# Retention, softplus MoE and routed MoE on one core: a third raw buffer inside the ring for the second matrix, all softplus of the second batch in pairs, halves of q in one operation

## The chip, the cores and the metric

The kernel runs on one core of a Trainium2 chip. The metric is device time in microseconds (us), the median of three runs. All times below come from the runs and the profiled execution of the kernel before, unless said otherwise.

## What is computed

Three layers in a row, all float32 at the borders. A retention attention (4 batches, 8 heads, 768 tokens, 64 per head) feeds a dense MoE layer with a softplus (3072 tokens, 512 to 2048 to 512), and this feeds a routed layer with 8 experts, one for each token.

```python
for t in range(S):
    state = gamma * state + einsum('bhd,bhe->bhde', k[:, :, t], v[:, :, t])
    y[:, :, t] = scale * einsum('bhd,bhde->bhe', q[:, :, t], state)
h = x @ w_in
g = maximum(h, 0) + log1p(exp(-abs(h)))
x2 = g @ w_out                                    # w_out is 2048 x 512
expert = argmax(x2 @ w_gate, axis=1)              # then one of 8 experts:
out[mask] = gate[mask] * (maximum(x2[mask] @ w1[e], 0) @ w2[e])
```

## The kernel before

Float32 factors are split into two float16 parts, hi and lo, and a product is three float16 matmuls (hi with hi, hi with lo, lo with hi). The attention goes by 24 chunks of 128 tokens, the dense layer by 8 batches of 384 tokens (three chunks each), the routed layer follows.

**Units.** The dense layer and the attention are written as one sequence of units. A batch has 16 units, one for each 128 columns of `w_in`; unit 16·ph + f is called by that number here. In each unit TensorE (PE) gets, in the order written: 12 matmuls 128x384 of the first matrix for batch ph (`l1_mm`, L890), the attention steps that are due (`at_step`), and 9 matmuls 128x512 of the second matrix (`l2_mm`, L938) for the batch before, four units late (`BACK`). So the second matmuls of batch 0 run in units 20 to 35; unit 20 + kk uses row block kk of `w_out`, and the nine are three token groups times (hi, hi), (hi, lo of `w_out`), (lo, hi). PE's order is the written one. The order on VectorE (DVE), ScalarE (ACT) and SyncE's DMA queue (SP) is set by a scheduler from the program and its priorities; SP is one in-order list (`in_line`).

**The second matrix.** `w_out` comes in eight blocks i = 0 to 7 of 1 MB, each for row blocks 2i and 2i+1. `load_out` (L667) loads a block, in a form that has to be put together from integers, into one of two raw tiles. `decode_out(i)`, written in unit 17 + 2i, first issues the loads up to block i+1, then runs `decode`: DVE L615, L617 and L619 in place on the raw tile, ACT L622 for the hi part, DVE L623 for the lo part. The results lie in `w1t`, which is part 1 of a large buffer (`ring`): per partition 8192 float16 elements of hi (u = 0) and then 8192 of lo (u = 1), a row block taking 512 of each.

**The softplus.** `softplus` (L893 to L920) takes a 128x384 block of PE's result through ACT (abs, relu, exp, ln), DVE L917, ACT L919 and DVE L920. For the units in the table `pairs` two blocks are held together and the later steps run once on 768 columns (DVE L903, L906). Batch 0 is all in pairs, of batch 1 the first four pairs; the other eight units of batch 1 run one by one.

**Attention steps.** For a chunk n: S(n), scores, then on DVE the masks L762 and the rests L764; Y(n), the products with them (L793), then Z, the state (L821 to L824), and on DVE L828, L829, L848 (the state) and L865 (the output's rest), after which SP transposes the output (L866) into `xt`, the input of a later batch. `at_prep` splits a loaded chunk (L713 to L720), and SP transposes it (L722). H is the step L840, once. `STEPS` says in which units of the first two batches the steps are written; in the second batch they are T6, S6, Y6, H6, S7, Y7, S8, Y8, in that order. The first six chunks use an older form (S L746, Y L800, Z L813, then L826 and L860 on DVE).

Of the kernel before, what the change touches and what calls it, by code (L numbers as in the profile page):

```python
# [8 lines left out]
F32 = mybir.dt.float32  # L9
F16 = mybir.dt.float16  # L10
U32 = mybir.dt.uint32
AF = mybir.ActivationFunctionType
ALU = mybir.AluOpType
# [7 lines left out]
P = 128  # L21
H = 8
D = 64
DM = 512
# [6 lines left out]
BT = 384  # L31
NB = NT // BT
CPB = BT // P
NF = FF // P
# [37 lines left out]
def moe_chain(ctx, tc, q, k, v, moe_w_in, moe_w_out, moe2_w_gate, moe2_w1, moe2_w2, cst, cst16, out, dbg=None):  # L72
    nc = tc.nc
# [41 lines left out]
    ring = wpool.tile([P, 4, 32, 512], F16, name="ring")  # L115
# [24 lines left out]
    def in_line(x):  # L140

        if queued[0] is not None:
            tc.add_manual_dep(x, queued[0].name, NOSYNC, reason="order")
        queued[0] = x
# [436 lines left out]
    with ExitStack() as pb, ExitStack() as pa:  # L581
# [5 lines left out]
        dd_stack = at_stack.enter_context(ExitStack())  # L587
        dd_p = dd_stack.enter_context(tc.tile_pool(name="dd", bufs=2, reuse_waits="tile"))
# [3 lines left out]
        def anchor(x):  # L592
            if now[0] is not None:
                tc.add_manual_dep(x.ins, now[0].name, NOSYNC, reason="order")
            return x
# [7 lines left out]
        def tick():  # L603
            for fn, args in events.pop(unit[0], []):
                fn(*args)
            unit[0] += 1
# [20 lines left out]
        BEHIND = {2: 3, 3: 4, 5: 5}  # L627
        LIN, LOUT = 4, 4
        BACK = 4
        STEPS = {0: (1, 2, 4, 5, 7, 9, 9, 11, 13), 1: (1, 3, 5, 6, 7, 9, 10, 13)}  # L630
        FILL = dict(T0=3,S0=2,z0=3,T1=2,S1=4,z1=5,y1=4,S2=6,z2=2)
        flat = ring[:, 2].rearrange("p a b -> p (a b)")
        dbuf = []
# [3 lines left out]
        def ahead(cnt, fn, upto):  # L637
            while cnt[0] < upto:
                fn(cnt[0])
                cnt[0] += 1  # L640

        nload = {"in": [0], "out": [0], "split": [0]}
# [19 lines left out]

        raws = {}

        def load_out(i):
            raws[i] = dd_p.tile([P, 2, DM, 2], U32, tag="raw", name="raw", bufs=2)
            in_line(nc.sync.dma_start(out=raws[i], in_=moe_w_out.rearrange("(k p) (f two) -> p k f two", p=P, two=2)[:, 2 * i:2 * i + 2]).ins)  # L667

        def decode_out(i):
            ahead(nload["out"], load_out, min(NF // 2, i + 2))  # L670
            hl = [w1t[:, u, 2 * i:2 * i + 2, :] for u in range(2)]
            decode(*hl, SWO, raws.pop(i))

# [25 lines left out]
        def at_prep(n):  # L699
            raw = raw_t.pop(n)  # L700
            if n < N32:
                tok_t[n] = raw
                return

            t = tbuf[n % 2]
            vh = at_p.tile([P, H, D], F16, tag="vh", name="vh")
            qv = t[:, 0:1024].rearrange("p (g x) -> p g x", g=4)
            qs = [[qv[:, :, 64 * (3 * half if u == 0 else half + 1):][:, :, 0:64] for half in range(2)] for u in range(2)]
            kv = t[:, 1024:2048].rearrange("p (h u d) -> p h u d", h=H, u=2)
            kl = t[:, 2048:2560].rearrange("p (h d) -> p h d", h=H)  # L710
            vl = t[:, 2560:3072].rearrange("p (h d) -> p h d", h=H)
            q4 = raw[:, 0].rearrange("p (g x) d -> p g x d", g=4)
            for half in range(2):  # L713
                anchor(nc.scalar.activation(out=qs[0][half], in_=q4[:, :, half], func=AF.Copy))
            anchor(nc.scalar.activation(out=kv, in_=raw[:, 2].unsqueeze(2).to_broadcast([P, H, 2, D]), func=AF.Copy))
            anchor(nc.scalar.activation(out=vh, in_=raw[:, 1], func=AF.Copy))
            for half in range(2):
                nc.vector.tensor_tensor(out=qs[1][half], in0=q4[:, :, half], in1=qs[0][half], op=ALU.subtract)
            nc.vector.tensor_tensor(out=kl, in0=raw[:, 2], in1=kv[:, :, 0], op=ALU.subtract)
            nc.vector.tensor_tensor(out=vl, in0=raw[:, 1], in1=vh, op=ALU.subtract)  # L720
            tT = at_p.tile([P, 20, P], F16, tag="tT", name="tT")
            nc.sync.dma_start_transpose(out=tT, in_=t[:, 0:2560])  # L722
            tok_t[n], trn_t[n] = (kv, kl, vh, vl), (tT[:, 0:8], tT[:, 8:16], tT[:, 16:20])
# [148 lines left out]
        spots = [[tbuf[i][:, u * 2 * wide:(u + 1) * 2 * wide] for u in range(2)] for i in range(2)]  # L872
        spots += [[flat[:, NF * BT * (u + 1) - 2 * wide * i:][:, 0:2 * wide] for u in range(2)] for i in (2, 1)]
        spots = [[x.bitcast(F32).rearrange("p (u t) -> p u t", u=2) for x in ar] for ar in spots]
        pairs = {(0, i): spots[3 if i == 7 else (i + 1) % 2] for i in range(8)}
        pairs.update({(1, i): spots[2 + i % 2] for i in range(4)})
        gt = {}
        pend = {}

# [175 lines left out]
        with tc.manual_schedule(engines={nc.tensor.engine}):  # L1055
# [75 lines left out]
            at_scale(CPB + 1)  # L1131
            for ph in range(NB + 1):
                ja, at_ = ph if ph < NB else None, min(ph + 2, NB)
                if ph == 2:
                    dd_stack.close()
                    rw_p = pb.enter_context(tc.tile_pool(name="rw", bufs=3, reuse_waits="tile", side="right"))
                    hl_stack = ExitStack()
                    hl_p = hl_stack.enter_context(tc.tile_pool(name="hl", bufs=2, reuse_waits="tile", side="right"))
                if ph == 7:
                    at_stack.close()  # L1140
                    hl_stack.close()
                    mb = pb.enter_context(tc.tile_pool(name="mb", bufs=2, reuse_waits="tile", side="right"))
                    sl = Slots(mb)
                    rx_p = pb.enter_context(tc.tile_pool(name="rx", bufs=3, reuse_waits="tile", side="right"))
                    late.extend((mb, mb.tile([P, P, 2], F32, tag="tb", name="tb", bufs=1), mb.tile([16, QP, 2], F32, tag="tq", name="tq", bufs=1)))
                if ph == 8:
                    sx_stack.close()
                    sl.pool = pa.enter_context(tc.tile_pool(name="mc", bufs=2, reuse_waits="tile"))
                attn = at_until(at_ * CPB)
                if ph in STEPS:  # L1150
                    attn = [STEPS[ph].count(f) for f in range(NF)]
                for f in range(NF if ph < NB else NF + BACK):
                    tick()
                    now_ = ph * NF + f
                    ph2, f2 = divmod(now_ - BACK, NF)
                    jb = ph2 - 1
                    LGD[0] = 5 if now_ >= NB * NF - 2 else 3
                    if ja is not None:
                        if ja == 0:
                            ahead(din, decode_in, min(NF, f + LIN + 1) // 2)  # L1160
                        l1_mm(ja, f)
                        with tc.high_priority(offset=150):
                            softplus()
                    if ja == 0:
                        if f == 9:
                            others()
                    if ph < 3:
                        ahead(dout, decode_out, min(NF, max(0, now_ - BACK - NF + LOUT + 1)) // 2)
                    for _ in range(attn[f] if ph < NB else 0):
                        at_step()  # L1170
                    if 3 * NF + BACK <= now_ < 7 * NF:
                        ahead(nsp, split, NSP * (now_ + 1 - 3 * NF - BACK) // (4 * NF - BACK))
                    if jb >= 0:
                        l2_mm(jb, f2 * 9, f2 * 9 + 9)
                    if ph2 == 2 and f2 == 10:
                        turns_pick()
                    if ph2 == 2 and f2 == 12:
                        es = experts(range(RING, E))
                        ahead(nload["split"], load_split, 2)
                    if ph2 == 7 and f2 == 7:  # L1180
                        early_pick()
                    if ph2 == 7 and f2 == 11:
                        early_spread()
                        for j in range(-NEARLY, 1 - NEARLY + 2):
                            sl.gather(j)
                    if ph2 == 7 and f2 == 13:
                        for j in range(-NEARLY, 1 - NEARLY + 2):
                            sl.turn(j)
                    if ph2 == 7:
                        if f2 == 5:  # L1190
                            direct = Direct([rw_p, rx_p], experts(range(RING)))
                        if f2 >= 6:
                            direct.at(9 * f2 + 9 - 9 * NF, last[0])
                    if ph2 == 8:
                        if f2 == 3:
                            sl.gather(-1)
                        direct.at(9 * f2 + 9, last[0])
# [158 lines left out]
```

## Time and profile before

| what | us |
|---|---|
| median of 3 runs | 879.53 (879.17 to 880.04) |
| profiled execution, whole time | 878.87 |
| its span, first to last instruction | 877.0 |
| PE busy | 863.2 (98%) |
| VectorE busy | 563.4 (64%) |
| ScalarE busy | 489.0 (56%) |
| PE busy from 100 to 120 / 120 to 140 / 140 to 160 | 18.31 / 18.41 / 20.00 |
| VectorE busy in the same stretches | 20.00 / 18.44 / 19.03 |

The profile is one execution, followed by the hardware profiler. Its whole time is 1.87 us above its span and 0.66 us under the median of the runs. A row of a timeline gives the start, the duration, the engine and the line; a matmul's row ends later than the next begins, since matmuls are pipelined, so times on PE are read here from start to start.

### The profile page before, as it was taken

The numbers are of one execution on the slowest core, as the hardware profiler recorded it, in microseconds if no ns is written. First come the engines' busy times: TensorE is split into PE (matmuls) and PEld (weight loads), VectorE is DVE, ScalarE is ACT, GpSimd is POOL, SyncE is SP. The second block draws the span as 40 slices with busy tenths as digits, with TensorE's granted clock in tenths as the row PEclk, the third lists the DMA queues.
The fourth block names the chain that finished last, engine by engine and source line by source line (L and its number), as shares of the span: only waits on it lengthen the run. The fifth ranks groups of instructions, "written<-read, shape, count | busy, mean of one in ns | idle before, by whom it ended". The sixth has DMA issues, their size and how long they took to land. (4 is left out here: it accounts for less than half of the span.)

```text
span 877.0 us, 17827 instructions
## 1 busy us (share of the span) xinstructions
PE 863.2 (98%) x6541; PEld 469.5 (54%) x6541; DVE 563.4 (64%) x1072; ACT 489.0 (56%) x882; POOL 92.9 (11%) x90
## 2 busy tenths in 40 slices
PE   9999999999999999999999999999999999999996
PEld 6666555555555555556555555544444444444453
DVE  6998998886798798799698645466633332221121
ACT  3688877765776777777676655455333332222220
POOL 0000000001010001001001001201332122212012
PEclk9999999999999999999999999999999999999998
DMA  9991982673779899698886412397699999889992
GB/s 251 252 286 48 222 198 82 148 136 73 181 195 223 209 247 219 192 250 203 229 188 171 124 49 70 107 273 204 153 234 209 208 198 216 225 205 249 300 281 57
DMA packets 281851, 165.87 MB, mean 189 GB/s; under 512 B 246914, under 2 KB 248331, under 8 KB 280738
## 3 DMA queue, kind: packets, MB, share of 16 engines
q1 hardware_dynamic: 276754, 151.49, 71.1%
q0 software_dynamic: 5008, 13.19, 5.3%
q8 instruction: 57, 0.93, 0.5%
q14 instruction: 32, 0.26, 0.1%
HBM read 135.01 MB, written 29.95 MB: 188 GB/s over the span
## 5 line engine op out<-in xcount | busy, mean ns | idle before, releaser
L890 PE MATMUL bank<-xt,ring 128*128 128x384 f16 x1536 | 268.9, 326 | 0.0
L938 PE MATMUL bank<-ring 128*128 128x512 f16 x1104 | 257.2, 379 | 1.6 <-DVE ring L623 1.6
L890 PEld LDWEIGHTS <-ring 128*128 128x128 f16 x1536 | 147.8, 98 | 104.4 <-issue 0.2
L938 PEld LDWEIGHTS <-ring 128*128 128x128 f16 x1152 | 109.4, 98 | 123.2 <-issue 2.3
L452 PE MATMUL h<-ring,xT 128*128 (+4 forms) x840 | 135.4, 361 | 0.0
L452 PE MATMUL bank<-ring,hT 128*128 (+5 forms) x864 | 135.0, 356 | 0.0
L485 ACT ACTIVATE r<-h 128x512 f32<-128x512 f32 (+1 forms) x51 | 30.1, 589 | 128.2 <-PE h L452 122.9
L452 PEld LDWEIGHTS <-hT 128*128 128x128 f16 (+2 forms) x864 | 62.9, 99 | 68.5 <-issue 2.5
L452 PEld LDWEIGHTS <-xT 128*128 128x128 f16 (+2 forms) x840 | 61.6, 98 | 68.7 <-issue 2.3
L910 ACT ACTIVATE a<-bank 128x384 f32<-128x384 f32 x104 | 50.8, 488 | 77.1 <-PE bank L890 77.0
L488 DVE TENSOR_TENSOR hb<-r,hb 128x512 f16<-128x512 f32 (+1 forms) x51 | 35.0, 686 | 83.6 <-ACT hb L487 83.4
L1026 POOL DMA_INDIRECT table<-row,pos x24 | 28.4, 1184 | 554.8 <-DVE pos L1009 512.6
L919 ACT ACTIVATE ring<-r 128x384 f16<-128x384 f32 x104 | 53.7, 519 | 45.7 <-DVE r L917 44.5
L914 DVE TENSOR_SCALAR r<-bank 128x384 f32<-128x384 f32 x96 | 53.1, 553 | 38.9 <-ACT a L910 38.0
L155 DVE SCALAR_TENSOR_TENSOR ring<-raw,ring 128x1024 f16<-128x1024 f32 x32 | 38.6, 1224 | 48.7 <-ACT ring L154 48.7
L920 DVE TENSOR_TENSOR ring<-r,ring 128x384 f16<-128x384 f32 x104 | 57.3, 552 | 18.9 <-ACT ring L919 18.7
L917 DVE SCALAR_TENSOR_TENSOR r<-a,r 128x384 f32<-128x384 f32 x104 | 57.3, 552 | 18.5 <-ACT a L916 18.1
L154 ACT ACTIVATE ring<-raw 128x1024 f16<-128x1024 f32 x32 | 33.0, 1052 | 51.4 <-DMA raw<-in_moe_w_dram 51.3
L916 ACT ACTIVATE a<-a 128x384 f32<-128x384 f32 x104 | 54.1, 520 | 2.2
L915 ACT ACTIVATE a<-a 128x384 f32<-128x384 f32 x104 | 54.0, 519 | 1.9
L522 DVE TENSOR_SCALAR o<-bank,gateT 128x512 f32<-128x512 f32 (+1 forms) x21 | 15.2, 724 | 51.0 <-PE bank L452 51.0
L155 DVE SCALAR_TENSOR_TENSOR hl<-raw,hl 128x1024 f16<-128x1024 f32 x32 | 39.1, 1220 | 4.7 <-ACT hl L154 3.9
(236 smaller groups left out, 936.3 us busy)
## 6 DMA issues: line engine op xcount, KB each, us to landing
ring<-wsp SPq DMA_DIRECT2D x28, 2048.0 KB
raw<-in_moe_w_dram SPq DMA_DIRECT2D x64, 512.0 KB
wsp<-hl SPq DMA_DIRECT2D x32, 512.0 KB
raw<-in_moe_w_out_dram SPq DMA_DIRECT2D x8, 1024.0 KB
ring<-in_moe_w_in_dram SPq DMA_DIRECT2D x7, 1024.0 KB
x2d<-xr SPq DMA_DIRECT2D x24, 256.0 KB
qkv<-in_q_dram SPq DMA_DIRECT2D x18, 256.0 KB
qkv<-in_k_dram SPq DMA_DIRECT2D x18, 256.0 KB
```

The source lines that it names most:

```text
L155: nc.vector.scalar_tensor_tensor(out=lo, in0=raw, scalar=SWE, in1=hi, op0=ALU.mult, op1=ALU.subtract).ins)
L452: ins = nc.tensor.matmul(ps[o, at_:at_ + width], lhsT=lhsT(u), rhs=rhs, start=first and at_ == 0, stop=last and ends).ins
L488: lo = nc.vector.tensor_tensor(out=hb[:, 1, hs], in0=r32, in1=hb[:, 0, hs], op=ALU.subtract)
L890: now[0] = nc.tensor.matmul(ps, lhsT=w0[:, u, kk, fs], rhs=x[:, kk, :], start=(m == 0), stop=(m == 11)).ins
L910: nc.scalar.activation(out=a, in_=ps, func=AF.Abs, scale=C1)
L914: nc.vector.tensor_scalar(out=r, in0=ps, scalar1=C1 * SG, scalar2=0.0, op0=ALU.mult, op1=ALU.max)
L915: nc.scalar.activation(out=a, in_=a, func=AF.Exp, scale=-1.0)
L916: nc.scalar.activation(out=a, in_=a, func=AF.Ln, bias=1.0)
L917: nc.vector.scalar_tensor_tensor(out=r, in0=a, scalar=SG, in1=r, op0=ALU.mult, op1=ALU.add)
L919: nc.scalar.activation(out=hi, in_=r, func=AF.Copy)
L920: nc.vector.tensor_tensor(out=lo, in0=r, in1=hi, op=ALU.subtract)
L938: last[0] = nc.tensor.matmul(l2[t], lhsT=gt[j][:, g, kk, t * P:(t + 1) * P], rhs=w1t[:, w, kk, :], start=(kk == 0 and p == 0), stop=(kk == ...
```

## The change

Five edits. (1) Blocks 2 and 5 of `w_out` get a third raw buffer, `own`: the last four row blocks' places of both halves of `w1t`, that is the elements 6144 to 8191 and 14336 to 16383 of ring part 1, which hold results only from block 6 on. With it `decode_out(i)` issues the loads up to block i+2; the loads of blocks 0 and 1 are written in unit 12, that of block 2 in unit 16. (2) All units of batch 1 run the softplus in pairs; the pairs 0 to 3 and 5 use the places that the first four had, the pairs 4, 6 and 7 two places in ring part 3, where batch 0's softplus results lay. (3) The hi part of q is one ACT operation and its lo part one DVE operation (L718 before) in place of two each. (4) `STEPS` of the second batch: Y7 goes from unit 25 to unit 26 and S8 from unit 26 to unit 27. (5) The pool of the raw tiles is closed, and two later pools are opened, at unit 33 instead of 32.

```diff
-        STEPS = {0: (1, 2, 4, 5, 7, 9, 9, 11, 13), 1: (1, 3, 5, 6, 7, 9, 10, 13)}
+        STEPS = {0: (1, 2, 4, 5, 7, 9, 9, 11, 13), 1: (1, 3, 5, 6, 7, 10, 11, 13)}
...
+        own = ring[:, 1].rearrange("p a b -> p (a b)").rearrange("p (u x) -> p u x", u=2)[:, :, 12 * DM:].bitcast(U32).rearrange("p k (s two) -> p k s two", two=2)
+
         def load_out(i):
-            raws[i] = dd_p.tile([P, 2, DM, 2], U32, tag="raw", name="raw", bufs=2)
+            raws[i] = own if i in (2, 5) else dd_p.tile([P, 2, DM, 2], U32, tag="raw", name="raw", bufs=2)
...
         def decode_out(i):
-            ahead(nload["out"], load_out, min(NF // 2, i + 2))
+            ahead(nload["out"], load_out, min(NF // 2, i + 3))
...
-            for half in range(2):
-                anchor(nc.scalar.activation(out=qs[0][half], in_=q4[:, :, half], func=AF.Copy))
+            anchor(nc.scalar.activation(out=qs[0], in_=q4, func=AF.Copy))
...
-            for half in range(2):
-                nc.vector.tensor_tensor(out=qs[1][half], in0=q4[:, :, half], in1=qs[0][half], op=ALU.subtract)
+            nc.vector.tensor_tensor(out=qs[1], in0=q4, in1=qs[0], op=ALU.subtract)
...
-        pairs.update({(1, i): spots[2 + i % 2] for i in range(4)})
+        read = [[ring[:, 3].rearrange("p a b -> p (a b)")[:, u * NF * BT + i * 4 * BT:][:, 0:4 * BT].bitcast(F32).rearrange("p (u t) -> p u t", u=2) for u in range(2)] for i in range(2)]
+        pairs.update({(1, i): spots[2 + i % 2] if i in (0, 1, 2, 3, 5) else read[i == 7] for i in range(8)})
...
+                    if now_ in (12, NF):
+                        ahead(nload["out"], load_out, 2 + now_ // NF)
```

What this does to the instructions is seen at three places. The lines from the softplus on have numbers higher by one after the change (L890 is L891, L938 is L939, L903 is L904, L906 is L907); the loads L667 and L686 are L669 and L688.

**Unit 21, PE and DVE.** PE before, at the second matmuls of unit 21 (`ring_88` is the ring, `bank1_70` the first token group's sums):

```order
L813 MATMUL z_1084<-qkv_521 64x64 x7
L938 LDWEIGHTS ring_88
L938 MATMUL bank1_70<-ring_88 128x512
L938 LDWEIGHTS ring_88
L938 MATMUL bank1_70<-ring_88 128x512
```

PE after, at the same place:

```order
L813 MATMUL z_1083<-qkv_521 64x64 x7
L939 LDWEIGHTS ring_88
L939 MATMUL bank1_70<-ring_88 128x512
L939 LDWEIGHTS ring_88
L939 MATMUL bank1_70<-ring_88 128x512 [waits DVE_49]
```

The order on PE is the same; the second of the nine matmuls, the one with the lo part of `w_out`, now waits for DVE. DVE before, around the decoding of block 2 (its raw tile is `raw_986`, that of block 1 `raw_928`):

```order
L720 TENSOR_TENSOR ring_88<-qkv_701,vh_1008 128x512
L615 TENSOR_SCALAR t_1064<-raw_986 128x1024
L906 TENSOR_TENSOR ring_88<-ring_88 128x768
L903 SCALAR_TENSOR_TENSOR ring_88<-ring_88 128x768
L623 SCALAR_TENSOR_TENSOR ring_88<-raw_928,ring_88 128x1024
L617 SCALAR_TENSOR_TENSOR raw_986<-raw_986,t_1064 128x1024
L826 SCALAR_TENSOR_TENSOR zz_130<-z_1084,cs_81 128x256
L906 TENSOR_TENSOR ring_88<-ring_88 128x768
L619 SCALAR_TENSOR_TENSOR raw_986<-raw_986 128x1024
```

DVE after (block 2 is now in the ring, and its L617 and L619 are the ones of form 128x2x512):

```order
L720 TENSOR_TENSOR ring_88<-qkv_701,vh_1009 128x512
L907 TENSOR_TENSOR ring_88<-ring_88 128x768
L904 SCALAR_TENSOR_TENSOR ring_88<-ring_88 128x768
L623 SCALAR_TENSOR_TENSOR ring_88<-raw_820,ring_88 128x1024
L615 TENSOR_SCALAR t_1063<-ring_88 128x1024
L907 TENSOR_TENSOR ring_88<-ring_88 128x768
L826 SCALAR_TENSOR_TENSOR zz_130<-z_1083,cs_81 128x256
L617 SCALAR_TENSOR_TENSOR ring_88<-ring_88,t_1063 128x2x512
L860 SCALAR_TENSOR_TENSOR xt_1073<-psY_1074,xt_1073 128x4x128
L904 SCALAR_TENSOR_TENSOR ring_88<-ring_88 128x768
L619 SCALAR_TENSOR_TENSOR ring_88<-ring_88 128x2x512
```

Block 2's L615 now stands behind block 1's L623, and L860 and a softplus step stand ahead of block 2's L619. That L619 is the operation that the matmul above waits for. PE's wait names only the engine; which operation it is follows from the count that the semaphore must reach.

**Unit 23, PE and SP.** PE after, at the second matmuls of unit 23 (before, no L938 of that unit waits):

```order
L758 MATMUL psS_1174<-tT_1016 128x128
L939 LDWEIGHTS ring_88
L939 MATMUL bank1_70<-ring_88 128x512
L939 LDWEIGHTS ring_88
L939 MATMUL bank1_70<-ring_88 128x512 [waits DMAHW2_49]
```

SP before, from the first block of `w_out` on:

```order
L667 DMA raw_926<-in_moe_w_out_dram 128x2x1024
L667 DMA raw_928<-in_moe_w_out_dram 128x2x1024
L667 DMA raw_986<-in_moe_w_out_dram 128x2x1024
L722 DMA_TRANSPOSE tT_1017<-ring_88 128x20x128
L686 DMA qkv_837<-in_q_dram 128x8x64
L686 DMA qkv_837<-in_k_dram 128x8x64
L686 DMA qkv_837<-in_v_dram 128x8x64
L686 DMA qkv_1070<-in_q_dram 128x8x64
L667 DMA raw_1062<-in_moe_w_out_dram 128x2x1024
```

SP after:

```order
L669 DMA raw_820<-in_moe_w_out_dram 128x2x1024
L669 DMA ring_88<-in_moe_w_out_dram 128x2x1024
L669 DMA raw_987<-in_moe_w_out_dram 128x2x1024
L722 DMA_TRANSPOSE tT_1016<-ring_88 128x20x128
L688 DMA qkv_841<-in_q_dram 128x8x64
L688 DMA qkv_841<-in_k_dram 128x8x64
L688 DMA qkv_841<-in_v_dram 128x8x64
L669 DMA raw_1061<-in_moe_w_out_dram 128x2x1024
L688 DMA qkv_1069<-in_q_dram 128x8x64
L688 DMA qkv_1069<-in_k_dram 128x8x64
L688 DMA qkv_1069<-in_v_dram 128x8x64
L669 DMA ring_88<-in_moe_w_out_dram 128x2x1024
```

The rows with `ring_88` are the loads of blocks 2 and 5 into `own`; the matmul of unit 23 waits for the second of them, which itself waits for block 2's L623 and for PE's second matmuls of unit 22.

**Unit 27, PE and DVE.** The second L939 matmul of unit 27 waits for DVE in the same way, and before it does not. DVE after, around block 5's decoding (L617 and L619 of form 128x2x512), from the state of chunk 7 on:

```order
L828 SCALAR_TENSOR_TENSOR zz_130<-z_1325,zz_130 128x512
L865 SCALAR_TENSOR_TENSOR ring_88<-psY_1284,ring_88 128x512
L615 TENSOR_SCALAR t_1390<-ring_88 128x1024
L718 TENSOR_TENSOR ring_88<-qkv_1069,ring_88 128x4x128
L829 TENSOR_TENSOR zz_130<-zz_130,cs_81 128x512
L719 TENSOR_TENSOR ring_88<-qkv_1069,ring_88 128x512
L617 SCALAR_TENSOR_TENSOR ring_88<-ring_88,t_1390 128x2x512
L720 TENSOR_TENSOR ring_88<-qkv_1069,vh_1396 128x512
L848 TENSOR_TENSOR z16_1352<-zz_130,z16_1352 128x512
L762 TENSOR_TENSOR ring_88<-psS_1405,cs_81 128x512
L762 TENSOR_TENSOR ring_88<-psS_1406,cs_81 128x512
L619 SCALAR_TENSOR_TENSOR ring_88<-ring_88 128x2x512
```

DVE before, around the same block:

```order
L829 TENSOR_TENSOR zz_130<-zz_130,cs_81 128x512
L762 TENSOR_TENSOR ring_88<-psS_1391,cs_81 128x512
L615 TENSOR_SCALAR t_1448<-raw_1262 128x1024
L762 TENSOR_TENSOR ring_88<-psS_1392,cs_81 128x512
L917 SCALAR_TENSOR_TENSOR r_1372<-a_1371,r_1372 128x384
L623 SCALAR_TENSOR_TENSOR ring_88<-raw_1156,ring_88 128x1024
L848 TENSOR_TENSOR z16_1342<-zz_130,z16_1342 128x512
L617 SCALAR_TENSOR_TENSOR raw_1262<-raw_1262,t_1448 128x1024
```

Block 5's L619 now stands behind both masks L762 of chunk 8. No operation of PE changes its place but Y7 with its state step, now in unit 26, and S8, now in unit 27; a second load wait is added in unit 20 (for block 2's load).

## Rows read from the trace of the kernel before

**Rows 1.** Waits of PE: engine, line, waited for; us in total, times, longest.

```profile
PE psY L793 <- DVE p L764: 1.7, 2, 0.9
PE bank L938 <- DVE ring L623: 1.6, 1, 1.6
```

**Rows 2.** PE's timeline, Y7 and Y8: start us, duration, line, count.

```profile
110.72 0.19 PE L793 MATMUL psY<-vh,p 128*128 128x64 f16 x1
...
114.73 1.47 PE L938 MATMUL bank<-ring 128*128 128x512 f16 x6
...
131.19 0.19 PE L793 MATMUL psY<-vh,p 128*128 128x64 f16 x1
...
133.17 1.47 PE L938 MATMUL bank<-ring 128*128 128x512 f16 x6
```

**Rows 3.** PE's timeline, second matmuls of unit 30 and first of unit 31.

```profile
137.07 0.38 PE L938 MATMUL bank<-ring 128*128 128x512 f16 x1
...
140.77 2.11 PE L890 MATMUL bank<-xt,ring 128*128 128x384 f16 x12
```

**Rows 4.** PE's timeline, units 21 to 24 (L890 opens a unit).

```profile
93.14 1.47 PE L938 MATMUL bank<-ring 128*128 128x512 f16 x6
...
95.09 2.11 PE L890 MATMUL bank<-xt,ring 128*128 128x384 f16 x12
...
100.10 2.11 PE L890 MATMUL bank<-xt,ring 128*128 128x384 f16 x12
102.05 0.61 PE L755 MATMUL psS<-tT 128*128 128x128 f16 x8
...
104.88 2.11 PE L890 MATMUL bank<-xt,ring 128*128 128x384 f16 x12
```

**Rows 5.** DVE's timeline around block 2's decoding (L615, L617, L619 in 90.77 to 96.58).

```profile
90.77 0.69 DVE L615 TENSOR_SCALAR t<-raw 128x1024 uint32<-128x1024 uint32 x1
91.37 0.95 DVE L906 TENSOR_TENSOR ring<-ring 128x768 f16<-128x768 f32 x1
...
93.11 1.23 DVE L623 SCALAR_TENSOR_TENSOR ring<-raw,ring 128x1024 f16<-128x1024 f32 x1
94.24 1.22 DVE L617 SCALAR_TENSOR_TENSOR raw<-raw,t 128x1024 uint32<-128x1024 uint32 x1
95.39 0.41 DVE L826 SCALAR_TENSOR_TENSOR zz<-z,cs 128x256 f32<-128x256 f32 x1
95.72 0.94 DVE L906 TENSOR_TENSOR ring<-ring 128x768 f16<-128x768 f32 x1
96.58 1.21 DVE L619 SCALAR_TENSOR_TENSOR raw<-raw 128x1024 uint32<-128x1024 uint32 x1
97.72 0.68 DVE L860 SCALAR_TENSOR_TENSOR xt<-psY,xt 128x512 f16<-128x512 f32 x1
98.32 0.94 DVE L903 SCALAR_TENSOR_TENSOR ring<-ring 128x768 f32<-128x768 f32 x1
```

**Rows 6.** SP's timeline, the issue of the last two blocks of `w_out`.

```profile
127.38 1.11 SPq L667 DMA_DIRECT2D raw<-in_moe_w_out_dram  x1
...
139.02 0.37 SPq L667 DMA_DIRECT2D raw<-in_moe_w_out_dram  x1
```

**Rows 7.** DVE's timeline, where these two are waited for, until their landing.

```profile
134.83 0.69 DVE L615 TENSOR_SCALAR t<-raw 128x1024 uint32<-128x1024 uint32 x1 [1.56 <-DMA raw<-in_moe_w_out_dram]
...
145.09 0.69 DVE L615 TENSOR_SCALAR t<-raw 128x1024 uint32<-128x1024 uint32 x1 [0.75 <-DMA raw<-in_moe_w_out_dram]
```

**Rows 8.** Windows: length, busy PE, PEld, DVE, ACT, POOL, then PEclk, DMA share, GB/s.

```profile
870.00:872.00 2.00, 0.00 (x0) 0.00 (x0) 0.00 (x0) 0.11 (x1) 0.20 (x1) 1.00 0.09 20
872.00:874.00 2.00, 0.00 (x0) 0.00 (x0) 0.00 (x0) 0.00 (x0) 0.77 (x1) 0.51 0.34 129
```

**Rows 9.** PE's timeline, the first matmuls of the program and the last.

```profile
1.22 3.38 PE L1092 MATMUL bank<-ring 128*128 128x384 f16 x10 [1.22 <-DVE ring L1087]
...
857.75 11.32 PE L452 MATMUL bank<-ring,hT 128*128 x200
```

More of the change, by code (lines that the diff above doesn't have):

```diff
@@ L707, in at_prep @@
             qv = t[:, 0:1024].rearrange("p (g x) -> p g x", g=4)
-            qs = [[qv[:, :, 64 * (3 * half if u == 0 else half + 1):][:, :, 0:64] for half in range(2)] for u in range(2)]
+            qs = [qv.rearrange("p g (x d) -> p g x d", d=64)[:, :, 0:4:3], qv.rearrange("p g (x d) -> p g x d", d=64)[:, :, 1:3]]
             kv = t[:, 1024:2048].rearrange("p (h u d) -> p h u d", h=H, u=2)
@@ L1133, in moe_chain @@
                 ja, at_ = ph if ph < NB else None, min(ph + 2, NB)
[L1134 to L1138, printed above, removed]
                 if ph == 7:
@@ L1157, in moe_chain @@
                     LGD[0] = 5 if now_ >= NB * NF - 2 else 3
+                    if now_ == 2 * NF + BACK - 3:
+                        dd_stack.close()
+                        rw_p = pb.enter_context(tc.tile_pool(name="rw", bufs=3, reuse_waits="tile", side="right"))
+                        hl_stack = ExitStack()
+                        hl_p = hl_stack.enter_context(tc.tile_pool(name="hl", bufs=2, reuse_waits="tile", side="right"))
                     if ja is not None:
```

## Prediction, made before the changed kernel ran

> **What bounds the kernel now.** PE is busy in 98% of the span, so only what makes PE wait, or gives it more to do, moves the time. I read the page's first part, then PE's waits, then PE's and DVE's timelines in the stretch that the change touches, from unit 20 (about 86 us) to unit 34 (about 152 us). In the list of waits two entries lie in this stretch [rows 1]: Y7 waits for the rests L764 on DVE, and the second matmuls of unit 30 wait for L623 of block 5. What each costs is better read from start to start. Y7 with its state step takes 114.73 − 110.72 = 4.01 us, the same step for chunk 8 takes 133.17 − 131.19 = 1.98 [rows 2]: 2.03 us are lost. The nine second matmuls of unit 30 take 140.77 − 137.07 = 3.70 [rows 3], those of unit 21 take 95.09 − 93.14 = 1.95 [rows 4]: 1.75 lost. Together 3.78 us; everything else that PE does between 100 and 160 us runs at its own pace.
>
> **What it removes.** Y7 a unit later has 3.9 us more before it needs L764; its loss of 2.03 goes. Block 5 is loaded far earlier and so decoded earlier; the loss of 1.75 in unit 30 goes. That is −3.78 us, if nothing else comes late.
>
> **What costs nothing.** The pairs of batch 1 and the single operations for q take instructions from ACT and DVE. Neither is on PE's path except where PE waits for a named operation; there their effect is in the counts below. The later opening of two pools moves no operation of this stretch. PE's own work is unchanged, instruction for instruction. The loads of blocks 0 and 1, moved to unit 12, and that of block 2, in unit 16, go where SP has nothing else to issue; the wait of unit 20 for block 2's load is met well ahead, since four units of 3.9 us and more lie between and a load takes 6 to 7.5 (below).
>
> **What it adds.** The new buffer takes the last quarter of the hi half and the last quarter of the lo half of `w1t`. Between these two lie the lo parts of row blocks 0 to 11. The order of the changed kernel shows that the matmul with the lo part, second of the nine, waits in units 21, 23 and 27 for something that was done to the buffer, though it reads none of it. I take the reason to be that a dependence is kept for the whole span from a buffer's first element to its last. The wait is built into the program, whatever its reason, so the question is only how late each is met.
>
> *Unit 21* waits for L619 of block 2. PE is ready at 93.14 + 0.22 = 93.36 (one matmul is 1.95/9 = 0.217) [rows 4]. DVE's new order has, from 90.77 on (the end of L720, where L615 starts before): two of 768 columns (L907, L904), L623 of block 1, L615, one of 768, L826, L617, L860, one of 768, and L619. From start to start a 768-wide one takes 0.87, L615 0.60, L623 1.13, L617 and L619 1.14, L826 0.33, L860 0.60, and L619 alone ends after 1.21 [rows 5]. 4 × 0.87 + 1.13 + 0.60 + 0.33 + 1.14 + 0.60 + 1.21 = 8.49, so L619 ends at 99.26. PE waits 99.26 − 93.36 = 5.9 us. Behind the waiting matmul stands the whole of PE. No DVE operation in that list needs anything that PE does after 93.36, so the wait doesn't feed itself.
>
> *Unit 23* waits for the load of block 5 into the same buffer. This load may start only when L623 of block 2 has read the buffer (99.26 + 0.87 + 1.13 = 101.3) and when PE has done the lo matmuls of unit 22, by the same span. After the first wait eight matmuls follow: unit 22 opens at 99.26 + 1.73 = 100.99, and unit 23 at 5.01 more [rows 4], 106.0; the lo matmuls of unit 22 end just ahead of that, at 105.9. The load's time from issue to landing is seen twice: 145.09 − 139.02 = 6.07 and 134.83 − 127.38 = 7.45 [rows 6, 7]. The second was issued behind three loads of a chunk, as SP's lateness shows; here the queue has been standing, so I take 6.07: it lands at 112.0. PE is ready at 106.0 + 1.95 + 0.87 + 0.22 = 109.0 (the twelve first matmuls take 102.05 − 100.10 = 1.95, and S7 104.88 − 102.05 less the second matmuls' 1.95 = 0.88 [rows 4]). It waits 3.0 us, 4.4 with the longer load. A shorter load than 6.07 is not seen; at 4.5 us the wait would be 1.4.
>
> The Trainium skill (DMA: Bandwidth & Descriptors, section "Anatomy of one DMA — SWDGE (gpsimd) path") gives a transfer about 2 us fixed and its bytes at 436 GB/s, which for 1 MB is an estimate of 4.4 us; by it the second wait would be 1.7 us shorter. It is told for GpSimd's path, and the two loads seen here are slower.
>
> *Unit 27* waits for L619 of block 5. Unit 24 opens at 112.0 + 1.73 = 113.7, units 25 and 26 after 3.9 each, 117.6 and 121.5; Y7 starts 1.95 later, at 123.45, and is over at 125.4 with its 1.98 [rows 2]. Then second matmuls, first matmuls of unit 27, S8: PE is ready at 125.4 + 1.95 + 1.95 + 0.88 + 0.22 = 130.4. DVE can start L828 when Y7's state is there, 125.4, and ahead of L619 stand L828, L865, L615, L718, L829, L719, L617, L720, L848 and two masks L762: ten at 0.60 like L860 and L615, and 1.14 [rows 5], then L619 with 1.21. 6.0 + 1.14 + 1.21 = 8.35, so L619 ends at 133.8 and PE waits 3.4 us.
>
> The sum: 5.9 + 3.0 + 3.4 − 3.78 = +8.5 us. Against the profiled execution (878.87) that is 887.4; the median of the runs stands 0.66 above that execution, so a median of 888.0.
>
> **The clock.** PE now stands still for 5.9 us once, and for 3.0 and 3.4. At the end of the program the last matmul is over at 857.75 + 11.32 = 869.07 [rows 9]; the granted clock is still 1.00 (the level of 2.4 GHz) in 870 to 872 and 0.51 (1.2 GHz) in 872 to 874 [rows 8]: it fell about 3 us after PE went idle. The first wait is twice that, so I count one fall. What a restart costs has one near row, the ten matmuls at the program's start: 3.38 us, where ten of the same form take 10/12 of 1.95 = 1.63 in unit 23 [rows 9, 4]. The clock column there reads 1.00, so the row doesn't prove the clock's share, but it is the only slow start of PE in the trace: 1.75 us for a fall. Bounds: 0 and three times 1.75 = 5.25, since the other two waits are near the 3 us.
>
> The Trainium skill (TensorE: Matmul & The Clock Gate, section "HAM oscillation — how this bites in real kernels") tells of kernels in which each burst of matmuls after a wait starts at the lower clock. By it each of the three waits would cost a fall. This trace has no wait of such a length but the program's end.
>
> With one fall: 8.5 + 1.75 = +10.25, 889.1 for such an execution and 889.8 as a median.
>
> **The rivals.**
> No fall: the clock rises at once, or doesn't fall in 5.9 us. 888.0.
> Two or three falls: 891.5 or 893.3.
> The waits are met in time, and a new late thing eats the gain. Then Y7 and unit 30 run free, Y8, two units behind S8 now instead of three, waits for L764 of chunk 8 behind block 5's decoding as Y7 did (2.0 us), and the first matmuls of unit 32 need chunk 8's output, which now passes L865 behind L623 of block 6 and a transposition. The two take back all but some 0.3 us: a median of 879.2, no change. This decides if L619 of block 2 ended before 93.4 us and the others by a like lead; with DVE busy without a gap from 90.77 to 99.2 [rows 5], that asks 5.9 us which I don't find. For it speaks only that the wait's target was read from counts. The point of balance is 3.78 us of waiting in all three.
> The change does what it is written for and nothing comes late: −3.78, a median of 875.7. It needs the same, and Y8 free too.
>
> **How the numbers follow.** One fall: 0.42 (889.8). No fall: 0.21 (888.0). Two or three: 0.22 (891.5 to 893.3). The waits met and the gain eaten: 0.09 (879.2). All gained: 0.05 (875.7). Rest 0.01. Of the sizes, the load's time moves it by −1.6 to +1.4, and DVE's order in unit 27 by about 1. The likeliest is 889.8; from 887.0 to 893.5 lies all of the slower cases but the shortest loads without a fall. A measurement can tell 0.2% (1.8 us) from no change: faster 0.05, same 0.10, slower 0.85.
>
> **What would show it.** In PE's list of waits after, the second matmul line should wait for DVE L619 twice (about 5.9 and 3.4 us) and for a load of `w_out` once (about 3.0), and the entries L764 and L623 [rows 1] should be gone. Unit 21's second matmuls should take about 7.9 us from start to start. The granted clock should fall below 1.00 between 97 and 103 us, and a unit behind it should take up to 1.75 us longer. DVE should show L619 of block 2 ending near 99. I am wrong if PE's second matmuls of unit 21 take 1.95 us as before, or if PE is at work while the wait stands in the program.

## The result: 893.2 us, 1.5% slower

The changed kernel takes 893.23 us (median of four runs, 890.56 to 893.61), the kernel before 879.78 beside it (four runs). The ratio is 1.0149, with a 95% interval of 1.0135 to 1.0163. The prediction was 889.8, in a range from 887.0 to 893.5; the sign, the places and the three waits (each within 0.9 us) were right, the share of the clock was too small.

The profile after is of an execution of 893.61 us with a span of 891.8. From its page, the busy times and the granted clock in 40 slices (each 22.3 us):

```profile
PE 869.4 (97%) x6541; PEld 471.3 (53%) x6541; DVE 563.8 (63%) x1047; ACT 486.3 (55%) x853; POOL 91.0 (10%) x90
...
PEclk9999899999999999999999999999999999999998
```

PE has 6.2 us more of busy time for the same 6541 matmuls, and the granted clock has an 8 in the fifth slice (89 to 111 us), where the kernel before has 9 in every slice but the last. The list of PE's waits (us in all, times, longest) shows where:

```profile
PE bank L939 <- DVE ring L619: 9.2, 2, 5.8
PE bank L939 <- DMA ring<-in_moe_w_out_dram: 1.9, 1, 1.9
...
PE rk L1004 <- DVE oh L994: 0.7, 1, 0.7
```

The two entries of [rows 1] are gone, the two that the prediction named have come: L619 of blocks 2 and 5 on DVE, and the load of block 5. PE's timeline at the three waits (start, duration, line, count; unit 21, unit 23, unit 27):

```profile
93.23 0.39 PE L939 MATMUL bank<-ring 128*128 128x512 f16 x1
99.47 2.29 PE L939 MATMUL bank<-ring 128*128 128x512 f16 x5 [5.85 <-DVE ring L619]
101.55 1.49 PE L939 MATMUL l<-ring 128*128 128x512 f16 x3
102.83 3.07 PE L891 MATMUL bank<-xt,ring 128*128 128x384 f16 x12
105.83 1.08 PE L840 MATMUL z<-zz,ident 128*64 128x256 f32 x8
...
111.62 0.39 PE L939 MATMUL bank<-ring 128*128 128x512 f16 x1
113.95 1.29 PE L939 MATMUL bank<-ring 128*128 128x512 f16 x5 [1.93 <-DMA ring<-in_moe_w_out_dram]
115.03 1.49 PE L939 MATMUL l<-ring 128*128 128x512 f16 x3
116.31 3.15 PE L891 MATMUL bank<-xt,ring 128*128 128x384 f16 x12
119.30 1.46 PE L939 MATMUL bank<-ring 128*128 128x512 f16 x6
...
133.84 0.39 PE L939 MATMUL bank<-ring 128*128 128x512 f16 x1
137.59 1.24 PE L939 MATMUL bank<-ring 128*128 128x512 f16 x5 [3.36 <-DVE ring L619]
138.66 1.25 PE L939 MATMUL l<-ring 128*128 128x512 f16 x3
139.70 3.40 PE L891 MATMUL bank<-xt,ring 128*128 128x384 f16 x12
142.94 1.46 PE L939 MATMUL bank<-ring 128*128 128x512 f16 x6
```

The matmul with the lo part stands still from 93.45 (one matmul of 0.22 after 93.23) to 99.47, from 111.84 to 113.95, and from 134.06 to 137.59: 6.02, 2.11 and 3.53 us. What comes behind each is slow. The eight second matmuls that are left take 3.36, 2.36 and 2.11 us in place of 1.73, and the twelve first matmuls of the next unit 3.00, 2.99 and 3.24 until the next row, in place of 2.04 (unit 22, ahead of H), 1.95 and 1.95. That is 2.59 + 1.67 + 1.67 = 5.93 us. The windows (length, busy time of PE, PEld, DVE, ACT, POOL, then PEclk, DMA share, GB/s) tell when the clock fell and rose:

```profile
96.00:97.00 1.00, 0.00 (x0) 0.00 (x0) 1.00 (x2) 0.00 (x0) 0.00 (x0) 1.00 1.04 366
97.00:98.00 1.00, 0.00 (x0) 0.00 (x0) 1.00 (x2) 0.00 (x0) 0.00 (x0) 0.97 0.97 385
98.00:99.00 1.00, 0.00 (x0) 0.00 (x0) 1.00 (x2) 0.69 (x1) 0.00 (x0) 0.50 1.06 319
104.00:105.00 1.00, 1.00 (x6) 0.48 (x4) 0.00 (x0) 0.00 (x0) 0.00 (x0) 0.62 0.00 0
114.00:115.00 1.00, 1.00 (x5) 0.43 (x5) 1.00 (x2) 1.00 (x3) 0.00 (x0) 1.00 1.20 237
115.00:116.00 1.00, 1.00 (x4) 0.42 (x3) 1.00 (x2) 1.00 (x2) 0.00 (x0) 0.50 1.05 196
118.00:119.00 1.00, 1.00 (x7) 0.53 (x6) 1.00 (x2) 0.00 (x0) 0.00 (x0) 0.79 1.27 241
...
138.00:139.00 1.00, 1.00 (x6) 0.51 (x5) 1.00 (x3) 1.00 (x2) 0.00 (x0) 0.95 1.19 267
139.00:140.00 1.00, 1.00 (x4) 0.31 (x3) 1.00 (x3) 0.45 (x1) 0.00 (x0) 0.50 1.37 267
142.00:143.00 1.00, 1.00 (x7) 0.57 (x6) 1.00 (x3) 0.00 (x0) 0.00 (x0) 0.85 0.03 7
```

With 1.00 and 0.50 as the two levels (2.4 and 1.2 GHz), the mean of the window in which it changed gives the moment: it fell at 97.9, while PE stood still, and at 115.0 and 138.9, when PE was at work again, and was back at 104.8, 118.4 and 142.3. Of this PE was at work for 5.3, 3.4 and 3.4 us; at half the clock half of each is lost, 2.6, 1.7 and 1.7, which is what the rows show.

The whole account, at the start of unit 33, which comes at 148.55 us before and at 162.44 after, 13.89 later: 6.02 + 2.11 + 3.53 = 11.66 of waits, 5.93 of the clock, less the 3.78 that the change removes, makes 13.81; the execution was 0.10 late already at unit 20. From unit 33 to the last unit of the dense layer at 559 us the two kernels run in step to 0.01 us. Another 0.84 us comes behind it, most of it in the ranks of the routed layer (the entry L1004 above; near 614 us in the kernel before, 629 here).

### The profile page after: what moved, and what is told of

The parts are those of the page before. It is cut to its first block, busy times and chain, and to the rows that moved or that the text cites. A ratio compares the mean times of both kernels' runs of the same rounds, so it can differ in the third digit from the quotient of the medians.

```text
span 891.8 us, 17768 instructions
## 1 busy us (share of the span) xinstructions
PE 869.4 (97%) x6541; PEld 471.3 (53%) x6541; DVE 563.8 (63%) x1047; ACT 486.3 (55%) x853; POOL 91.0 (10%) x90
## 5 line engine op out<-in xcount | busy, mean ns | idle before, releaser
L891 PE MATMUL bank<-xt,ring 128*128 128x384 f16 x1536 | 272.2, 329 | 0.0
L939 PE MATMUL bank<-ring 128*128 128x512 f16 x1104 | 258.7, 380 | 11.1 <-DVE ring L619 9.2
L891 PEld LDWEIGHTS <-ring 128*128 128x128 f16 x1536 | 149.1, 99 | 107.4 <-issue 5.2
L939 PEld LDWEIGHTS <-ring 128*128 128x128 f16 x1152 | 109.9, 98 | 134.1 <-issue 14.3
L911 ACT ACTIVATE a<-bank 128x384 f32<-128x384 f32 x96 | 46.9, 488 | 72.1 <-PE bank L891 71.4
L920 ACT ACTIVATE ring<-r 128x384 f16<-128x384 f32 x96 | 49.8, 519 | 47.0 <-DVE r L918 45.8
L921 DVE TENSOR_TENSOR ring<-r,ring 128x384 f16<-128x384 f32 x96 | 53.1, 554 | 19.6 <-ACT ring L920 19.4
L918 DVE SCALAR_TENSOR_TENSOR r<-a,r 128x384 f32<-128x384 f32 x96 | 53.1, 553 | 18.7 <-ACT a L917 18.4
L917 ACT ACTIVATE a<-a 128x384 f32<-128x384 f32 x96 | 49.9, 520 | 2.1
L916 ACT ACTIVATE a<-a 128x384 f32<-128x384 f32 x96 | 49.9, 519 | 2.0
```

The source lines that it names most:

```text
L891: now[0] = nc.tensor.matmul(ps, lhsT=w0[:, u, kk, fs], rhs=x[:, kk, :], start=(m == 0), stop=(m == 11)).ins
L911: nc.scalar.activation(out=a, in_=ps, func=AF.Abs, scale=C1)
L916: nc.scalar.activation(out=a, in_=a, func=AF.Exp, scale=-1.0)
L917: nc.scalar.activation(out=a, in_=a, func=AF.Ln, bias=1.0)
L918: nc.vector.scalar_tensor_tensor(out=r, in0=a, scalar=SG, in1=r, op0=ALU.mult, op1=ALU.add)
L920: nc.scalar.activation(out=hi, in_=r, func=AF.Copy)
```

## The experiments

All are read at the same two points: where unit 33 opens (148.55 us before) in the profile, and the median beside runs of the kernel before on the same chip.

| run | median | before beside it | ratio, 95% interval | unit 33 opens against before |
|---|---|---|---|---|
| strips | 878.99 | 879.07 | 0.9995 (0.9982 to 1.0008) | −1.58 |
| filled waits | 889.12 | 879.07 | 1.0121 (1.0098 to 1.0144) | +8.70 |
| no buffer | 879.90 | 879.07 | 1.0009 (0.9990 to 1.0027) | −0.71 |
| buffer only | 896.98 | 879.07 | 1.0206 (1.0185 to 1.0228) | +16.43 |
| block 2 only | 880.38 | 880.05 | 1.0002 (0.9991 to 1.0012) | +0.26 |
| strips, Y8 later | 877.55 | 880.05 | 0.9969 (0.9957 to 0.9982) | −3.30 |
| block 2 only, Y8 later | 878.31 | 880.05 | 0.9983 (0.9974 to 0.9993) | −3.88 |
| before, PE 1.95 us later | 881.91 | 880.05 | 1.0026 (1.0015 to 1.0036) | 0.00, +1.95 from unit 38 on |
| strips, Y8 later, PE 1.95 us later | 879.40 | 879.57 | 0.9999 (0.9987 to 1.0011) | −3.35, −1.39 from unit 38 on |
| strips, Y8 later, again | 878.27 | 879.57 | 0.9982 (0.9970 to 0.9994) | −3.58 |

**Strips.** Does the wait come from the span between the buffer's two strips? Each strip holds one row block of a raw block. Here blocks 2 and 5 are loaded, and decoded, one strip at a time; buffer, loads and all else stay.

```diff
+            if i in (2, 5):
+                raws[i] = own
+                for k in range(2):
+                    in_line(nc.sync.dma_start(out=own[:, k:k + 1], in_=src[:, 2 * i + k:2 * i + k + 1]).ins)
+                return
...
-            decode(*hl, SWO, raws.pop(i))
+            raw = raws.pop(i)
+            for k in ((0, 1), (1, 2)) if i in (2, 5) else ((0, 2),):
+                decode(*(x[:, k[0]:k[1]] for x in hl), SWO, raw[:, k[0]:k[1]])
```

> The changed kernel, but blocks 2 and 5 are loaded and decoded in two operations each, one for each strip of the buffer, so that no operation spans the lo parts of row blocks 0 to 11. Theory (the waits come from the span from the first to the last element): the waits of units 21, 23 and 27 are gone, the granted clock stays at 1.00 between 90 and 150 us, and the time falls by the 11.7 us of waits and the 6.0 us of clock less what comes late next: about 879 if Y8 waits for L764 of chunk 8 by 2 us and unit 32 for its input, as the rival of the prediction has it, 875.5 if neither does. Rival (the waits come from the buffer's place in the second matrix itself, or from the earlier loads): the three waits stay, 890 to 893.

Measured 878.99, no difference to before that can be told. PE's waits and unit 21 on its timeline:

```profile
PE psY L801 <- DVE p L772: 1.9, 1, 1.9
PE rk L1012 <- DVE oh L1002: 1.6, 1, 1.6
```

```profile
93.30 1.47 PE L947 MATMUL bank<-ring 128*128 128x512 f16 x6
...
95.25 2.11 PE L899 MATMUL bank<-xt,ring 128*128 128x384 f16 x12
...
131.56 0.20 PE L801 MATMUL psY<-vh,p 128*128 128x64 f16 x1 [1.87 <-DVE p L772]
```

The same run on DVE, the last operation in place on block 2:

```profile
99.47 0.70 DVE L619 SCALAR_TENSOR_TENSOR ring<-ring 128x512 uint32<-128x512 uint32 x1
```

The nine second matmuls of unit 21 take 95.25 − 93.30 = 1.95, and no second matmul waits for DVE or a load of `w_out`; the granted clock is 1.00 from 90 to 150 us. The wait is not only met sooner, it is gone: this L619 ends at 100.17, later than in the changed kernel (99.41), when the nine matmuls are long done. The same data in the same place, touched in two pieces, costs no wait: what waited was the span. And the third rival of the prediction comes true in its first half: with the waits gone, Y8 waits for L764 of chunk 8 (L772 in this run's numbering), 1.9 us; DVE has no free moment from 90 to 130 us (20.00 busy of 20 from 90 to 110 and from 110 to 130). Its second half, the late input of unit 32, does not come.

**Filled waits.** What is the clock's share? Idle matmuls fill the three waits of the changed kernel.

```diff
+                if j == 0 and t == 0 and p == 1:
+                    for _ in range({1: 36, 3: 12, 7: 21}.get(kk, 0)):
+                        nc.tensor.matmul(banks[0][:, 0:BT], lhsT=w0[:, 0, 0, 0:P], rhs=w0[:, 0, 0, 0:BT], start=True, stop=True)
                 last[0] = nc.tensor.matmul(l2[t], lhsT=gt[j][:, g, kk, t * P:(t + 1) * P], rhs=w1t[:, w, kk, :],
```

> The changed kernel with idle matmuls of the first matmuls' form ahead of the waiting matmul: 36 in unit 21, 12 in unit 23, 21 in unit 27 (5.9, 2.0 and 3.4 us at full clock), on a bank that is overwritten afterwards. They fill the waits and add nothing to the results. Theory (6.0 us of the loss are the clock, 11.7 the waits): PE's waits are filled, the granted clock stays at 1.00, the units 22, 24 and 28 run at 1.95 for their first twelve matmuls, and the time is 887 to 888. Rival (the slow units after the waits are slow for another reason, such as DVE and the loads on the same memory): 12 first matmuls still take 3.0 us there, 892 to 894.

Measured 889.12, a little over the range given and clearly under 892. PE's timeline (L941 are the idle matmuls) and one window:

```profile
93.49 6.01 PE L941 MATMUL bank<-ring 128*128 128x384 f16 x36
99.50 1.24 PE L942 MATMUL bank<-ring 128*128 128x512 f16 x5
100.58 0.81 PE L942 MATMUL l<-ring 128*128 128x512 f16 x3
101.23 2.11 PE L891 MATMUL bank<-xt,ring 128*128 128x384 f16 x12
103.27 1.08 PE L840 MATMUL z<-zz,ident 128*64 128x256 f32 x8
```

```profile
95.00:100.00 5.00, 5.00 (x31) 2.85 (x30) 5.00 (x7) 2.11 (x4) 0.00 (x0) 1.00 1.06 308
100.00:105.00 5.00, 5.00 (x31) 2.44 (x30) 3.35 (x5) 2.10 (x5) 0.00 (x0) 1.00 0.40 86
```

The clock stays at 1.00 in all windows from 90 to 150, and the first matmuls of unit 22 take 2.04, not 3.00. Unit 33 opens 13.89 − 8.70 = 5.19 us earlier than in the changed kernel. The wait of unit 27 was longer here by 0.73 (4.26 from the first idle matmul to the next second matmul, against 3.53), so the clock's share is 5.92 us, beside the 5.93 read from the slow rows. Slow matmuls are the clock's, not a matter of traffic.

**No buffer.** The changed kernel without the buffer and the earlier loads (the three places undone); pairs, q and the steps' new units stay.

> The changed kernel without the third raw buffer and with the loads of before (two blocks ahead); pairs, the single operations for q and the new units of Y7 and S8 stay. Theory (all of the loss is the buffer): no waits in units 21, 23 and 27, clock 1.00, Y7 runs free (2.0 us gained), unit 30 waits for block 5 as before or less: 876 to 879.5. Rival (pairs or the new order of the attention steps cost something too): over 881.

Measured 879.90, no difference. No wait in units 21, 23 and 27, clock 1.00 from 90 to 150. Unit 33 opens 0.71 earlier than before, though this execution was 0.92 late from its start: 1.6 us are gained, as with strips. Pairs, q and steps cost nothing in this stretch, and the buffer is not needed for what they gain: unit 30 did not wait for block 5 here either. Y8 waits 1.8 us for L764 (L762 in this run's numbering).

**Buffer only.** The kernel before with the buffer and the earlier loads alone.

```diff
+            raws[i] = own if i in (2, 5) else dd_p.tile([P, 2, DM, 2], U32, tag="raw", name="raw", bufs=2)
+            ahead(nload["out"], load_out, min(NF // 2, i + 3))
+                    if now_ in (12, NF):
+                        ahead(nload["out"], load_out, 2 + now_ // NF)
```

> The kernel before with the third raw buffer and the earlier loads alone; softplus, q and STEPS as before. Theory: the same three waits, some 6, 2 to 3 and 2 to 5 us, with clock falls after each, 889 to 895. Rival (the waits are long only because pairs and the moved steps have changed DVE's order): waits under 3 us in all, under 884.

Measured 896.98, over the expected 895. PE's waits:

```profile
PE bank L940 <- DVE ring L619: 11.6, 2, 5.9
PE bank L940 <- DMA ring<-in_moe_w_out_dram: 1.9, 1, 1.9
```

The same three waits, 5.9, 1.9 and 5.7 us, and three falls of the clock. The third is 2.3 us longer than in the changed kernel (5.66 against 3.36). So the buffer carries the whole loss, and the other edits shorten it: with them block 5's L619 comes sooner (it ends at 137.53, here at 139.35).

**Block 2 only.** One contiguous piece of the lo half, for block 2; block 5 in a raw tile.

```diff
-            raws[i] = own if i in (2, 5) else dd_p.tile(
+        own = ring[:, 1].rearrange("p a b -> p (a b)")[:, 24 * DM:].bitcast(U32).rearrange("p (k s two) -> p k s two", k=2, two=2)
+            raws[i] = own if i == 2 else dd_p.tile(
```

> The changed kernel with one contiguous piece as third buffer, the elements 12288 to 16383 of ring part 1 (the last half of the lo parts), for block 2 alone; block 5 goes into one of the two raw tiles again. Nothing is split, and no lo part lies between the buffer's ends that is read before block 4 is decoded. Theory of the span: no wait in units 21, 23 and 27, clock 1.00, unit 33 opens 1 to 4 us earlier than in the kernel before, and the time is 876 to 879.5, as in the run with strips. Rival (a buffer inside the second matrix costs waits wherever it lies): 884 or more.

Measured 880.38, under the rival's 884 and just over the range. No wait in units 21, 23 and 27. Only the one of unit 21 is put to the test here, since the other two hung on block 5, which has a raw tile again: with nothing that is read between its ends, a buffer inside the second matrix costs no wait there. The gain of Y7 is there as well (unit 28 opens 2.0 us earlier than at unit 20's lead, with strips and here), and Y8 takes it back: it waits 1.6 and 0.3 us for L764, and the clock is at 0.50 from 134 to 136.

**Y8 later.** With strips Y8 was the next thing late; here `STEPS` ends with 14 in place of 13, with strips and with block 2 alone.

```diff
-1: (1, 3, 5, 6, 7, 10, 11, 13)}
+1: (1, 3, 5, 6, 7, 10, 11, 14)}
```

> The run with strips, and Y8 in unit 30 instead of 29. There Y8 waited 1.9 us for L764 of chunk 8. Theory: that wait goes; unit 33 opens 3.5 us earlier than in the kernel before, if chunk 8's output is still in time for unit 32, else the 1.9 us come back as a wait of unit 32. If the end of the program follows PE: 875.5 to 877; if it takes the gain back, as it took 2.1 us in the profile of the run with strips: 878 to 879.

> The run with block 2 alone, and Y8 in unit 30. DVE has four small operations less than with strips. Expected as the run before: unit 33 opens 3 to 4 us earlier, 875.5 to 877 if the end follows PE, 878 to 879 if not.

Strips with Y8 in unit 30: 877.55, and 878.27 when taken again; both intervals end below 1. Unit 33 opens 3.3 to 3.6 us earlier; 0.34 us are lost in unit 32, whose second matmuls wait for block 6. With block 2 alone nothing in the stretch waits any more, unit 33 opens 3.88 us earlier, 3.79 of them since unit 20, which is the 3.78 of the two losses, and the time is 878.31. These versions beat the kernel before, by 0.2 to 0.3%. The medians lie above the forecast for an end that follows PE (875.5 to 877), two of the three in the one for an end that doesn't (878 to 879): by the medians the end keeps back 1 to 2 us of what the stretch gains.

**Does the end follow PE?** Twelve idle matmuls on PE, 1.95 us, in unit 37 (the first text below says unit 39), once in the kernel before and once in the best version.

> The kernel before with 12 idle matmuls of the first matmuls' form ahead of the second matmuls of unit 39, 1.95 us of PE that nothing hides there. It asks whether the end of the program follows PE. Theory (PE's time reaches the end one to one): 881.0 to 881.6, that is 1.95 over the kernel before. Rival (the loads of the routed layer's weights set a later part of the end, whatever PE's lead): between 879.1 and 880.5.

> The run with strips and Y8 in unit 30, with the 12 idle matmuls in unit 37 as in the run on the kernel before: PE reaches the end of the dense layer 1.4 us earlier than the kernel before instead of 3.3. Theory (the end of the program takes back part of an early arrival, because a load of the routed layer's weights is waited for there, and nothing of a late one): less than 1.95 us over the same kernel without the idle matmuls, 0 to 1.2 us. Rival (the end follows PE one to one, and what came back before was chance): 1.95 us over it.

> The run with strips and Y8 in unit 30 once more, beside the run above on the same chip: 876.5 to 878.5, and in its profile again a wait of about 1.5 us in the ranks of the routed layer (PE for DVE).

The kernel before goes from 880.05 to 881.91, 1.86 of the 1.95 (1.3 to 3.2 by the interval), just over the range of the theory and clearly over the rival's 880.5: there the end follows PE. The best version goes from 878.27 to 879.40, 1.1 us. In the profiles of this pair it is 2.19 at the last dense unit and 3.07 at the last matmul, so the medians and the two profiles don't agree; 0.8 of it is a longer wait for an input of the routed layer (1.1 us in place of 0.3).

In the profiles the versions with Y8 later lose 3.0 to 3.5 us between the last dense unit and the last matmul against the kernel before, the strips 2.1. Of this 1.7 are lost at the ranks near 614 us, most of it in one wait (L1004 or its like, 1.4 to 1.6 us in every version with strips or with block 2 alone, 1.2 with filled waits and without the buffer, 0.7 after, 0.2 with the buffer only, none in the kernel before); 0.3 to 0.9 just ahead of it, where the input is waited for; the rest, up to 0.9, in short pauses behind 700 us. The kernel before with the idle matmuls loses 1.0 in such pauses too, so this last part isn't the versions' own. PE's timeline at the ranks, in the best version when taken again, and in the kernel before:

```profile
612.80 0.18 PE L1012 MATMUL rk<-oh,cs 128*128 128x8 f16 x1 [1.54 <-DVE oh L1002]
```

```profile
614.22 0.17 PE L1003 MATMUL rk<-oh,cs 128*128 128x8 f16 x1
```

Ahead of this wait ACT waits for a load of the routed layer's weights. ACT's timeline, in the best version the first time, and in the kernel before (start, duration, then idle time and its cause):

```profile
602.72 1.06 ACT L154 ACTIVATE ring<-raw 128x1024 f16<-128x1024 f32 x1 [9.49 <-DMA raw<-in_moe_w_dram]
```

```profile
603.22 1.06 ACT L154 ACTIVATE ring<-raw 128x1024 f16<-128x1024 f32 x1 [6.17 <-DMA raw<-in_moe_w_dram]
```

The last loads of these weights ahead of it were issued from 593.25 on in the one and from 596.55 on in the other. If it is the first of them, it took 9.5 us in place of 6.7: issued 3.3 us sooner, it landed 0.5 sooner. Behind it on ACT and DVE stand the last outputs of the dense layer. Why this load takes longer in these versions no run here shows; it stays open, as does whether the 1.1 us is a share given back or chance.

## Why the prediction was right, and where it was not

*What it removes:* right. Y7 with its state goes from unit 26's first matmuls at 125.14 to 129.06 together in 3.92, 1.97 for itself, and unit 30's second matmuls take 154.65 − 152.71 = 1.94. The 3.78 us are gained, and as the strips show, only as long as nothing is next; with the waits gone Y8 is next.

*The wait of unit 21:* 5.9 forecast, 6.02 measured. DVE did what the sum had, to the operation:

```profile
90.80 0.95 DVE L907 TENSOR_TENSOR ring<-ring 128x768 f16<-128x768 f32 x1
...
98.19 1.22 DVE L619 SCALAR_TENSOR_TENSOR ring<-ring 128x1024 uint32<-128x1024 uint32 x1
```

L907 starts at 90.80 (90.77 in the sum), L619 ends at 99.41 (99.26).

*The wait of unit 23:* 3.0 forecast, 2.11 measured, the one of the three that is off. The load of block 5 is on SP's timeline at 108.78, the moment at which unit 23 opens, as the step had it. From there to the matmul at 113.95 are 5.2 us, where I took 6.07 from [rows 6, 7]. The step that failed is the load's time; I had no shorter load in the trace, and gave 1.4 as the wait for one of 4.5. The estimate of 4.4 from the Trainium skill (DMA: Bandwidth & Descriptors, section "Anatomy of one DMA — SWDGE (gpsimd) path") lies below the measured 5.2; the two loads of the rows, 6.07 and 7.45, lie above it.

*The wait of unit 27:* 3.4 forecast, 3.53 measured. From the end of Y7's state at 129.06 to the end of L619 are 8.47 us, where the sum has 8.35:

```profile
136.32 1.21 DVE L619 SCALAR_TENSOR_TENSOR ring<-ring 128x1024 uint32<-128x1024 uint32 x1
```

*The clock:* this is the term that was mis-sized: one fall of 1.75 forecast, three falls of 2.59, 1.67 and 1.67 measured, 5.93 in all, and 5.92 by the run with filled waits. Two steps failed. I counted a fall only for a wait well over the 3 us that passed at the program's end until the clock fell, and PE's waits of 2.11 and 3.53 brought one each; the second and third fell when PE was at work again (at 115, 1.1 us after the matmuls had gone on, and near 139). And the price of 1.75, from the slow start of the program, fits the two shorter waits (1.67) but not the first (2.59), where PE was at work at the lower level from 99.47 to 104.8, longer than behind the others. The length of the wait doesn't set this price: in the run with the buffer only the first wait is as long (5.9 us), and its second matmuls and the first matmuls behind it lose 1.7.

The rival with three falls, 893.3 us, is what came; that the median, 893.23, meets it so closely is luck, since its waits are 0.6 too long and its falls 0.7 too cheap. The Trainium skill (TensorE: Matmul & The Clock Gate, section "HAM oscillation — how this bites in real kernels") tells of a kernel in which each burst behind a wait starts at the lower clock. This trace agrees with that in the count, three falls for three waits, and in the start for the first wait alone: behind the other two the matmuls went on at 1.00 and the clock fell 1.1 and 1.3 us later. I gave two or three falls 0.22. In one of the four runs the time was 890.56, 2.7 less; a fall that did not happen would account for that, but no trace of that run is here, and its mean clock, 0.991 beside 0.989, 0.993 and 0.990 of the others, does not tell.

*The sum:* 8.5 forecast without the clock, 11.66 − 3.78 = 7.88 measured; with the clock 10.25 and 13.81.

*The rival in which the gain is eaten* (0.09) was right in what it said of Y8 and wrong in unit 32: the strips, which are that rival's case, give 878.99 where it said 879.2, but by another sum, 1.6 gained at unit 33 and about as much lost at the end.

*The reason given for the waits*, the span from first to last element, is shown by the strips and by block 2 alone.

## What to carry to other kernels

A buffer made of two pieces of a larger one may be guarded as the whole span between them; whoever reuses strips should touch them one at a time, or look in the built order for waits on instructions that the edit does not mention, and price each by who it waits for. A wait of PE can cost more than its length: here 11.7 us of waits brought 5.9 us of a lower clock with them, and the price lies behind the wait, in matmuls that wait for nothing. Idle matmuls in the waits showed which part was the clock's. Where an engine is full (DVE from 90 to 130 us), taking one stall away shows the next; move the step that is next late as well.

## What the runs showed of the hardware

That the clock can fall after waits under 1 us was not expected. In the kernel before with 12 idle matmuls in unit 37, Y7 waits as in the kernel before, 0.82 and 0.89 us, long ahead of the idle matmuls. The clock falls behind it (windows with PEclk as the third number from the end):

```profile
112.00:114.00 2.00, 1.11 (x34) 1.00 (x35) 2.00 (x3) 1.70 (x5) 0.00 (x0) 1.00 1.20 242
114.00:115.00 1.00, 1.00 (x30) 0.91 (x26) 1.00 (x3) 0.68 (x2) 0.00 (x0) 0.67 0.48 87
115.00:116.00 1.00, 1.00 (x10) 0.49 (x11) 1.00 (x2) 1.00 (x4) 0.00 (x0) 0.50 0.52 66
...
117.00:118.00 1.00, 1.00 (x4) 0.36 (x3) 1.00 (x3) 0.82 (x2) 0.00 (x0) 0.63 1.03 422
```

In the profile of the kernel before the same waits brought no fall. The second matmuls behind Y7 took 3.15 us in place of 1.95 and the loss of 1.6 us was gone again when unit 31 opened, since the wait of unit 30 shrank by as much. Two other runs show the same at Y8: without the buffer it waits 1.54 and 0.28 us and the clock stays at 1.00 from 130 to 140; with block 2 alone it waits 1.57 and 0.28 us, and the clock is at 0.50 from 133 to 136. So whether a short wait brings a fall differs from one execution to the next, what decides it stays open, and part of the cost can hide behind a later wait.
